# A transformer block in float32 on one core: the output projection regrouped into eleven matmuls a tile, with later weight splits

## The chip, the cores and the metric

The kernel runs on one core of one Trainium2 chip. The time is device microseconds of one launch, the median of three runs. One further launch was recorded by the hardware profiler; all rows below are of that one.

TensorE (PE) multiplies, VectorE (DVE) and ScalarE (ACT) do elementwise work, GpSimd (POOL) does small columns and issues accumulating DMAs, and SyncE (SP) issues the other DMAs. Each engine runs its own queue in the order in which the program was written.

## The reference

```python
x = A_x                                     # (1, 2048, 448), float32
mod = silu(c) @ w_mod                       # six rows of 448: sa, ca, ga, sb, cb, gb
h = layernorm(x) * (1 + ca) + sa
q, k, v = heads(h @ wqkv)                   # 16 heads of 28
pq, pk = phi(q), phi(k)                     # phi(t) = (t + 1 if t > 0 else exp(t)) + 1e-6
kv, z = einsum(pk, v), sum(pk)              # per head, over the 2048 tokens
o = (pq @ kv) / (pq . z + 1e-6)
x = x + ga * (o @ wo)
h = layernorm(x) * (1 + cb) + sb
u = gelu(layernorm(h).T @ w1 + b1)          # the MLP mixes tokens: w1 is 2048 x 1792
x = x + gb * (u @ w2 + b2).T                # w2 is 1792 x 2048
```

## The kernel before

The 2048 tokens are sixteen tiles of 128 rows. Everything is float32, but a matmul at full rate takes rounded operands. So an operand is split: a high part, rounded by ScalarE into a float32r tile, and a low part, the rest, by a VectorE subtraction. A product is then three matmuls: high by high, high by low, low by high.

**Stages.** First keys, queries and the sums over tokens, then a second loop over the tiles, then the rest of the MLP. The change is in the second loop and just ahead of it.

**Ahead of the loop.** The per-head matrices `kvm` (masked to the heads) times the four row groups `wo_sb[g]` of 112 rows give four products `wp` of 112 by 448, so that division by the denominator, `kv` and `wo` become one matrix. Each is split from PSUM into `wph` (ScalarE) and `wpl` (VectorE), eight tiles on 112 partitions.

**The loop.** It has `NT + LAG` = 21 iterations. Iteration `i` works on several tiles at once, in this order in the program (the function names are those of the code):

- TensorE: `b_transpose(i)` turns the normalised queries `pn` of tile `i` into a PSUM bank `tq`; `b_out(i-1)` is the output projection of the tile before, into `op`; `a_q` projects one or more of the queries still left (`QS` says how many in which iteration, one where it says nothing); `step(0, i-5)` is a piece of the first MLP matmul: four output tiles `up` by three matmuls.
- ScalarE and VectorE: `b_high(i)` and `b_low(i)` split `tq` into `pth` and `ptl`; `b_res(i-2)` adds `op` to x; `b_prod`, `b_sum`, `b_recip`, `b_scale` make `pn` of tile `i+1`; `b_norm1_a`, `b_norm1_b` (tile `i-3`) and `b_norm2` (tile `i-4`, which makes `y` and `h2h` on ScalarE) are the two layer norms; `b_mean1` and `b_mean2` are sums of squares on ScalarE (`sqa`, `sqb`); `b_low2` makes `h2l`; `a_phi_q` ends the queries with two activations and one VectorE operation.
- GpSimd: `nb` (in `b_norm2`), `nm` (`b_mean1`), `den` (`b_eps`), `ny` (`b_mean2`), and `b_rstd`, which is `vw` and the power `rt`, in that order within an iteration. `b_norm1_b` and `b_norm2` of the next iteration use `rt`.
- w1: `load_to` queues loads of 128 by 512 pieces `pr` on SP, `split_to` splits the next of them. A piece in `PIECE_DMA` is split without VectorE: ScalarE makes the high part `ph` and its negative in `pl`, and a GpSimd DMA adds the piece onto `pl`.

`step(0, t)` needs piece `t`; from iteration 17 on the loop also begins the next group of columns, with pieces 16 to 19. The tiles come from two pools of buffers, 74 in one and 27 in the other. The second holds among others the query weights (until the last `a_q`), `pd`, `pn`, the `wp` parts and the parts of pieces 9 to 11.

At the end of an iteration the program has:

```python
a_phi_q(nq)
load_to(14 + (i + 1) // 2)
split_to(10 + (i + 1) // 2)
if res or norm1:
    b_rstd(i, 0 if res else 1, 2 if norm1 else 1)
```

Of the kernel before, what the change touches and what calls it, by code (L numbers as in the profile page):

```python
# [8 lines left out]
F32 = mybir.dt.float32  # L9
F32R = mybir.dt.float32r  # L10
AF = mybir.ActivationFunctionType
# [3 lines left out]
P = 128  # L15
S, D, F = 2048, 448, 1792
NT = S // P
NF = F // P
G = 112
# [1 line left out]
DH = 28  # L21
EPS = 1e-5

PIECE_DMA = range(14, 18)
PRE_LOAD = {14: 2, 15: 4}
KV_LAG = 4
HIGH_AT = {13: (11, 12), 14: (13,), 15: (14, 15)}
# [10 lines left out]
CUT2 = {2: 9, 3: 9, 4: 8, 5: 7}  # L38
LAG = 5
MOD_AT = {9: [(4, 0)], 10: [(4, 1)], 11: [(4, 2)], 12: [(4, 3)], 13: [(3, 0)], 14: [(3, 1)]}  # L40
QS = {0: 2, 4: 2}
WARM = 9
PRE = 9
MID = 5
# [6 lines left out]
def block_kernel(ctx: ExitStack, tc: tile.TileContext, x, xt, wqkv, wo, w1, b1, w2, b2, c, wmod, wfirst, out):  # L51
    nc = tc.nc
# [15 lines left out]
    def slot(name, w=D, dt=F32, parts=P):  # L68
        return slots.tile([parts, w], dt, name=name, tag="slot", padded_shape=[P, 512])

    def tslot(name, dt=F32, parts=P, w=D):
        return tok.tile([parts, w], dt, name=name, tag="tok", padded_shape=[P, 512])


    def moving(new, name, dt=F32R, parts=P):
        return new(name, dt=dt, parts=parts, w=512)[:, 16:16 + D]
# [4 lines left out]
    def split(full, hi, lo):  # L81
        nc.scalar.activation(hi, full, AF.Copy)  # L82
        nc.vector.tensor_sub(lo, full, hi.bitcast(F32))  # L83
# [6 lines left out]
    ident = cst.tile([P, P], F32, name="ident")  # L90
# [103 lines left out]
    def mod_out(j, ps):  # L194
        mods[j] = cst.tile([P, D], F32, name=f"mod{j}")
        nc.scalar.activation(mods[j], ps[:, :D], AF.Copy, bias=1.0 if j == 4 else 0.0)
# [48 lines left out]
    def mod_sum2(j):  # L245
        ps = bank(f"modp{j}")
        hi, lo = macc.pop(j)
        nc.tensor.matmul(ps[:, :D], ones_r[:G, :], hi, start=True, stop=False)
        nc.tensor.matmul(ps[:, :D], ones_r[:G, :], lo, start=False, stop=True)
        return ps  # L250
# [46 lines left out]
    raws, parts = {}, {}  # L297
    done = {"load": 0, "split": 0}

    def load_to(i):  # L300
        while done["load"] < min(i, len(pieces)):
            k = done["load"]
            t, m, f0, n = pieces[k]
            raws[k] = slot(f"pr{k}", 512)
            nc.sync.dma_start(raws[k].rearrange("p (t f) -> p t f", t=m),
                              w1[t * P:(t + m) * P, f0 * P:(f0 + n) * P].rearrange("(t p) f -> p t f", p=P))
            done["load"] += 1

    def split_to(i):
        while done["split"] < min(i, len(pieces)):  # L310
            k = done["split"]
            new = tslot if k in TOKP else slot
            hi, lo = new(f"ph{k}", dt=F32R, w=512), new(f"pl{k}", dt=F32R, w=512)
            if k in PIECE_DMA:
                full = raws.pop(k)
                nc.scalar.activation(hi, full, AF.Copy)
                nc.scalar.activation(lo, hi.bitcast(F32), AF.Copy, scale=-1.0)
                nc.gpsimd.dma_start(lo, full, accum_op=ALU.add)
            else:
                split(raws.pop(k), hi, lo)  # L320
            parts[k] = (hi, lo)
            done["split"] += 1
# [64 lines left out]
    tps = {}  # L387
# [52 lines left out]
        nc.vector.scalar_tensor_tensor(dst, e, 1.0, r, op0=ALU.min, op1=ALU.add)  # L440
        return dst

    def phi_q(ps, t):
        dst, e, r = slot(f"pq{t}"), slot(f"eq{t}"), slot(f"rq{t}")
        nc.scalar.activation(e, ps, AF.Exp, scale=mv[t][:, 2:3])
        nc.scalar.activation(r, ps, AF.Relu, scale=mv[t][:, 2:3])
        nc.vector.scalar_tensor_tensor(dst, e, 1.0, r, op0=ALU.min, op1=ALU.add)
        return dst

    pq = [None] * NT  # L450
    qps = {}

    def a_q(t):
        project(t, 0, "qp")
        qps[t] = close(t, 0)
        del heads[t]

    def a_phi_q(keep=0):
        for t in sorted(qps)[:len(qps) - keep]:
            pq[t] = phi_q(qps.pop(t), t)  # L460


    xss, pks = {}, {}
# [267 lines left out]
    mp = mod_sum2(3)  # L731
    load_to(PRE + MID + 3)
    split_to(8)
    Wph, Wpl = [], []


    H2h, H2l = [None] * NT, [None] * NT
# [15 lines left out]
    def b_recip(t):  # L753
        nc.vector.reciprocal(dens[t], dens[t])

    def b_scale(t):
        pn = tslot(f"pn{t}")
        nc.vector.scalar_tensor_tensor(pn.rearrange("p (h d) -> p h d", d=DH),
                                       pq[t].rearrange("p (h d) -> p h d", d=DH), 1e-6,
                                       dens.pop(t).unsqueeze(2).to_broadcast([P, H, DH]),  # L760
                                       op0=ALU.add, op1=ALU.mult)
        pns[t] = pn
        pq[t] = None

    def b_transpose(t):
        pn = pns.pop(t)
        tps[t] = bank(f"tq{t}")
        for g in range(4):
            nc.tensor.transpose(tps[t][:G, g * P:(g + 1) * P], pn[:, g * G:(g + 1) * G], ident)  # L769

    def b_high(t):
        phs[t] = (slot(f"pth{t}", 512, F32R, parts=G), slot(f"ptl{t}", 512, F32R, parts=G))
        nc.scalar.activation(phs[t][0], tps[t][:G, :], AF.Copy)  # L773

    def b_low(t):
        nc.vector.tensor_sub(phs[t][1], tps.pop(t)[:G, :], phs[t][0].bitcast(F32))

    def b_out(t):
        ph, pl = phs.pop(t)
        opb[t] = bank(f"op{t}")  # L780
        n = 0
        for g in range(4):
            s = slice(g * P, (g + 1) * P)
            for a, b in ((ph, Wph[g]), (ph, Wpl[g]), (pl, Wph[g])):
                nc.tensor.matmul(opb[t][:, :D], a[:, s], b, start=(n == 0), stop=(n == 11))  # L785
                n += 1

    def b_sums(i):
        if i not in vss:
# [3 lines left out]
    def b_res(t):  # L793
        sums[t] = small.tile([P, 1], F32, name=f"sm{t}", tag="sm")
        nc.vector.scalar_tensor_tensor(X[t], opb.pop(t)[:, :D], 1.0, X[t], op0=ALU.mult, op1=ALU.add,
                                       accum_out=sums[t])
# [20 lines left out]
    def b_rstd(i, lo, hi):  # L817
        ve = small.tile([P, 2], F32, name=f"vw{i}", tag="vw")
        nc.gpsimd.tensor_scalar(ve[:, lo:hi], vss.pop(i)[:, lo:hi], 1.0 / D, EPS, op0=ALU.mult, op1=ALU.add)
        rss[i] = small.tile([P, 2], F32, name=f"rt{i}", tag="rt")  # L820
        nc.gpsimd.tensor_tensor(rss[i][:, lo:hi], ve[:, lo:hi], mhalf[:, lo:hi], op=ALU.pow)
# [10 lines left out]
    def b_low2(t):  # L832
        nc.vector.tensor_sub(H2l[t], ys.pop(t), H2h[t].bitcast(F32))
# [17 lines left out]
    for g in range(4):  # L851
        wp = bank(f"wp{g}")
        nc.tensor.matmul(wp[:G, :D], kvm[:, g * G:(g + 1) * G], wo_sb[g], start=True, stop=True)  # L853
        hi, lo = moving(tslot, f"wph{g}", parts=G), moving(tslot, f"wpl{g}", parts=G)
        split(wp[:G, :D], hi, lo)
        Wph.append(hi)
        Wpl.append(lo)
    mod_out(3, mp)

    accs, early = None, []  # L860
    for i in range(NT + LAG):
        if i == NT - 4:
            load_mod(5)
        if NT - 3 <= i <= NT:
            mod_part(5, i - NT + 3)
        if i == NT:
            mod_split(5)
        if i < NT:
            b_transpose(i)
        if 0 <= i - 1 < NT:  # L870
            b_out(i - 1)
        nq = min(len(late), QS.get(i, 1))
        for _ in range(nq):
            a_q(late.pop(0))
        t = i - LAG
        mp = mod_sum2(5) if i == NT else None
        if t >= 0:
            if t == 0:
                accs = [bank(f"up{f}") for f in range(4)]
            if i > NT:  # L880
                if not early:
                    early = [bank(f"up{W1G[1][0] + f}") for f in range(W1G[1][1])]
                r = i - NT - 1
                step(W1G[1][0], r, early, H2h[r], H2l[r])
            step(0, t, accs, H2h[t], H2l[t])
        if mp is not None:
            mod_out(5, mp)
        if i < NT:
            b_high(i)
        scale, res, norm1, norm2 = i + 1 < NT, 0 <= i - 2 < NT, 0 <= i - 3 < NT, 0 <= i - 4 < NT  # L890
        if res:
            b_res(i - 2)
        if scale:
            b_prod(i + 1)
        if norm2:
            b_norm2(i - 4, i)
        if res:
            b_mean1(i - 2, i)
        if norm1:
            b_norm1_a(i - 3)  # L900
        if scale:
            b_sum(i + 1)
        if norm1:
            b_norm1_b(i - 3, i)
        if scale:
            b_eps(i + 1)
        if i < NT:
            b_low(i)
        if norm1:
            b_mean2(i - 3, i)  # L910
        if scale:
            b_recip(i + 1)
        if scale:
            b_scale(i + 1)
        if norm2:
            b_low2(i - 4)
        a_phi_q(nq)
        load_to(14 + (i + 1) // 2)
        split_to(10 + (i + 1) // 2)
        if res or norm1:  # L920
            b_rstd(i, 0 if res else 1, 2 if norm1 else 1)

# [303 lines left out]
```

## Time and profile before

| | us |
|---|---|
| median of 3 runs | 444.76 (444.47 to 445.54) |
| the profiled launch, its own time | 445.22 |
| its span, first to last instruction | 443.5 |
| TensorE busy | 436.6 (98%), 2392 matmuls |
| VectorE busy | 364.7 (82%), 811 instructions |
| ScalarE busy | 273.3 (62%), 572 instructions |
| GpSimd busy | 110.0 (25%), 195 instructions |

The granted TensorE clock is at full speed in all of the span's forty slices. The second loop runs from 117.06 us, where tile 0 is transposed, to about 229 us, where the first four `up` are done. An engine's busy time counts instructions that overlap their neighbours at both ends, so what an engine needs is read from the distance between starts. An idle time of an engine that is not the one being waited for costs nothing.

### The profile page before, as it was taken

Reading aid. Unit: us, or ns where it says so; the run is one execution under the profiler, and the core shown is the slowest. Engines: PE = TensorE matmul, PEld = TensorE weight load, DVE = VectorE, ACT = ScalarE, POOL = GpSimd, SP = SyncE. Lnnn points to the kernel's source line nnn. Section 1 sums busy time; section 2 is a strip of 40 time slices with the busy share of each in tenths; the row PEclk is TensorE's granted clock in tenths of the full one; section 3 lists DMA queues with packets and bytes.
Section 4 is the critical chain, followed back from the end, with each engine's and each line's share of the span. In section 5 each row is a group of like instructions: output and inputs, shape, how many; then the busy total and the mean of one; then the engine's idle time right before and its main releaser. Section 6 shows DMA issues by size and latency. Waiting matters only on the chain.

```text
span 443.5 us, 7249 instructions
## 1 busy us (share of the span) xinstructions
PE 436.6 (98%) x2392; PEld 404.4 (91%) x2392; DVE 364.7 (82%) x811; ACT 273.3 (62%) x572; POOL 110.0 (25%) x195
## 2 busy tenths in 40 slices
PE   8999999999999999999999999999999999999995
PEld 7878899999899999989999999999999999999995
DVE  3989996689998899896468975829699998898892
ACT  3889877648656776767664354617375555645550
POOL 3227563200025355554300000010102331132010
PEclk9999999999999999999999999999999999999999
DMA  7998999545100004322328652478369978995332
GB/s 256 381 290 171 237 225 217 106 152 173 58 0 1 24 25 102 67 49 47 120 63 249 220 165 89 138 201 225 68 190 206 207 171 176 216 184 112 61 41 43
DMA packets 62294, 63.47 MB, mean 143 GB/s; under 512 B 4720, under 2 KB 54576, under 8 KB 62256
## 3 DMA queue, kind: packets, MB, share of 16 engines
q1 hardware_dynamic: 54048, 49.79, 37.3%
q0 software_dynamic: 8208, 13.21, 18.9%
q8 instruction: 19, 0.31, 0.3%
q14 instruction: 19, 0.16, 0.1%
HBM read 45.88 MB, written 7.34 MB: 120 GB/s over the span
## 4 chain that ended last, share of the span: by engine, by line
PE 93%; ACT 3%; DVE 2%; POOL 1%; issue 1%; ACTq 0%
PE y L1024 19%; PE up L838 10%; PE up L837 10%; PE up L836 9%; PE y L1025 9%; PE cacc L514 7%; PE qp L420 7%; PE op L785 7%; PE kp L420 6%; PE tq L769 1%; PE col L218 1%; PE warm L181 1%; PE qp L427 1%; PE kvb L725 1%; PE rowb L283 1%; PE wp L853 1%
## 5 line engine op out<-in xcount | busy, mean ns | idle before, releaser
L838 PE MATMUL up<-h2h,pl 128*128 128x448 f32 x224 | 81.4, 364 | 0.0
L837 PE MATMUL up<-h2l,ph 128*128 128x448 f32 x224 | 81.3, 363 | 0.0
L836 PE MATMUL up<-h2h,ph 128*128 128x448 f32 x224 | 80.9, 361 | 0.0
L986 POOL DMA_DIRECT2D a<-a x16 | 14.1, 960 | 142.7 <-DVE u L950 76.9
L837 PEld LDWEIGHTS up<-h2l,ph 128*128 128x128 f32 x224 | 42.1, 188 | 3.2
L836 PEld LDWEIGHTS up<-h2h,ph 128*128 128x128 f32 x224 | 42.0, 187 | 2.9
L838 PEld LDWEIGHTS up<-h2h,pl 128*128 128x128 f32 x224 | 42.1, 188 | 2.3
L83 DVE TENSOR_TENSOR pl<-pr,ph 128x512 fp32r<-128x512 f32 x52 | 34.6, 686 | 3.1 <-ACT ph L82 2.3
L82 ACT ACTIVATE ph<-pr 128x512 fp32r<-128x512 f32 x52 | 31.2, 626 | 3.3 <-PE up L837 2.6
L1030 ACT ACTIVATE cc<-y 128x448 f32<-128x448 f32 x24 | 12.9, 544 | 23.7 <-PE y L1025 23.7
L1044 POOL DMA_DIRECT2D out_dram<-yt x15 | 13.6, 908 | 48.6 <-DVE yt L1035 38.1
L514 PE MATMUL cacc<-pkh,xh 128*128 128x448 f32 x64 | 24.4, 382 | 0.3 <-ACT pkh L488 0.3
L785 PE MATMUL op<-wph,pth 112*128 112x448 f32 x64 | 24.5, 382 | 0.0
L950 DVE TENSOR_TENSOR u<-u,mod 128x448 f32<-128x448 f32 x14 | 8.7, 621 | 18.8 <-ACT u L949 18.6
L514 PE MATMUL cacc<-pkl,xh 128*128 128x448 f32 x64 | 23.3, 364 | 0.2 <-DVE pkl L490 0.2
L949 ACT ACTIVATE u<-up,b1c 128x448 f32<-128x448 f32 x14 | 8.7, 624 | 23.9 <-PE up L838 21.9
L420 PE MATMUL kp<-wh,hh 128*128 128x448 f32 x64 | 23.2, 373 | 0.2 <-ACT wh L256 0.2
L420 PE MATMUL qp<-wh,hh 128*128 128x448 f32 x64 | 23.3, 364 | 0.0
L785 PE MATMUL op<-wpl,pth 112*128 112x448 f32 x64 | 23.2, 363 | 0.0
L785 PE MATMUL op<-wph,ptl 112*128 112x448 f32 x64 | 23.2, 363 | 0.0
L773 ACT ACTIVATE pth<-tq 112x512 fp32r<-112x512 f32 x16 | 9.6, 598 | 17.3 <-PE tq L769 17.3
L827 ACT ACTIVATE y<-y,nb,rt 128x448 f32<-128x448 f32 x16 | 12.1, 758 | 11.8 <-POOL nb L826 11.8
(231 smaller groups left out, 1357.9 us busy)
## 6 DMA issues: line engine op xcount, KB each, us to landing
pr<-in_B_w_dram SPq DMA_DIRECT2D x56, 256.0 KB, 3.1
a<-in_B_w_dram SPq DMA_DIRECT2D x32, 256.0 KB, 4.8
a<-in_B_w_dram SPq DMA_DIRECT2D x32, 192.0 KB, 4.7
xt<-in_xt_dram SPq DMA_DIRECT2D x16, 256.0 KB, 4.8
x<-in_A_x_dram SPq DMA_DIRECT2D x16, 224.0 KB, 4.8
out_dram<-x SPq DMA_DIRECT2D x15, 224.0 KB, 2.5
out_dram<-yt POOLq DMA_DIRECT2D x15, 224.0 KB, 5.2
wm<-in_B_wmod_dram SPq DMA_DIRECT2D x16, 196.0 KB, 4.8
```

Of the source, the lines that this page charges most:

```text
L82: nc.scalar.activation(hi, full, AF.Copy)
L83: nc.vector.tensor_sub(lo, full, hi.bitcast(F32))
L420: nc.tensor.matmul(pps[t, j][:, :D], a[:, ch * P:(ch + 1) * P], w, start=first, stop=False)
L514: nc.tensor.matmul(cacc[ch][:, :D], a[:, s], b, start=(t == 0 and i == 0), stop=(t == NT - 1 and i == len(todo) - 1))
L785: nc.tensor.matmul(opb[t][:, :D], a[:, s], b, start=(n == 0), stop=(n == 11))
L836: nc.tensor.matmul(ps[:, :D], hi[:, sl], mh, start=first, stop=False)
L837: nc.tensor.matmul(ps[:, :D], hi[:, sl], ml, start=False, stop=False)
L838: nc.tensor.matmul(ps[:, :D], lo[:, sl], mh, start=False, stop=last)
L986: nc.gpsimd.dma_start(w, a, accum_op=ALU.add)
L1024: nc.tensor.matmul(ps[:, :D], h[:, s], w, start=opens and r == 0, stop=False, skip_group_check=True)
L1025: nc.tensor.matmul(ps[:, :HD], l[:, s], wh, start=False, stop=closes and r == PAIRS - 1, skip_group_check=True)
L1044: nc.gpsimd.dma_start(of[t * P:(t + 1) * P, :], ysum.pop(t), accum_op=ALU.add)
```

## The change

- **Products onto 128 partitions.** The 448 rows of the combined matrix are taken as three chunks of 128 rows and one of 64 instead of four of 112. `b_transpose` transposes chunks of 128, 128, 128 and 64 columns. The last chunk's high part stands on partitions 0 to 63 and its low part on 64 to 127 of the same columns, so that its high and low parts are multiplied in one matmul: eleven matmuls a tile instead of twelve.
- For that `b_high` and `b_low` become two instructions each (`b_low_last` is the second of VectorE's).
- **The combined matrix** is copied by ScalarE from PSUM into `wpg`, moved by eight SP DMAs between buffers into four tiles `wpr` with the new rows (the last 64 rows twice), and split from there in `wp_split`, at the end of iteration 0.
- **w1's pieces** are split later, and pieces 8 to 17 by DMA (14 to 17 before). One piece is split in each iteration from 6 on. Loads are as before up to iteration 15 and go further ahead after it.
- **Order:** `b_rstd` comes ahead of `split_to`; the queries' two activations come right after `b_high`, their VectorE operation at the end as before; three `a_q` in iteration 0 and one in iteration 4 (two and two before); `mod_sum2(5)` comes after `step` in iteration 16; `b_res(15)` comes in iteration 16.

```diff
-PIECE_DMA = range(14, 18)
+PIECE_DMA = range(8, 18)
-QS = {0: 2, 4: 2}
+QS = {0: 3}
...
     def b_transpose(t):
         pn = pns.pop(t)
         tps[t] = bank(f"tq{t}")
-        for g in range(4):
-            nc.tensor.transpose(tps[t][:G, g * P:(g + 1) * P], pn[:, g * G:(g + 1) * G], ident)
+        for ch in range(3):
+            nc.tensor.transpose(tps[t][:, ch * P:(ch + 1) * P], pn[:, ch * P:(ch + 1) * P], ident)
+        nc.tensor.transpose(tps[t][:64, 384:], pn[:, 384:D], ident)
 
     def b_high(t):
-        phs[t] = (slot(f"pth{t}", 512, F32R, parts=G), slot(f"ptl{t}", 512, F32R, parts=G))
-        nc.scalar.activation(phs[t][0], tps[t][:G, :], AF.Copy)
+        phs[t] = (slot(f"pth{t}", 512, F32R), slot(f"ptl{t}", 384, F32R))
+        nc.scalar.activation(phs[t][0][:, :384], tps[t][:, :384], AF.Copy)
+        nc.scalar.activation(phs[t][0][:64, 384:], tps[t][:64, 384:], AF.Copy)
 
     def b_low(t):
-        nc.vector.tensor_sub(phs[t][1], tps.pop(t)[:G, :], phs[t][0].bitcast(F32))
+        hi, lo = phs[t]
+        nc.vector.tensor_sub(lo, tps[t][:, :384], hi[:, :384].bitcast(F32))
+
+    def b_low_last(t):
+        ps, hi = tps.pop(t), phs[t][0]
+        nc.vector.tensor_sub(hi[64:, 384:], ps[:64, 384:], hi[:64, 384:].bitcast(F32))
 
     def b_out(t):
...
-        for g in range(4):
-            s = slice(g * P, (g + 1) * P)
-            for a, b in ((ph, Wph[g]), (ph, Wpl[g]), (pl, Wph[g])):
-                nc.tensor.matmul(opb[t][:, :D], a[:, s], b, start=(n == 0), stop=(n == 11))
-                n += 1
+        for ch in range(3):
+            s = slice(ch * P, (ch + 1) * P)
+            todo += [(ph[:, s], Wph[ch]), (ph[:, s], Wpl[ch]), (pl[:, s], Wph[ch])]
+        todo += [(ph[:, 384:], Wph[3]), (ph[:, 384:], Wpl[3])]
...
-        hi, lo = moving(tslot, f"wph{g}", parts=G), moving(tslot, f"wpl{g}", parts=G)
-        split(wp[:G, :D], hi, lo)
...
+        wpg = tslot(f"wpg{g}", parts=G)
+        nc.scalar.activation(wpg, wp[:G, :D], AF.Copy)
...
+                    nc.sync.dma_start(Wpr[ch][p0 + r0 - ch * P:p0 + r1 - ch * P], wpg[r0 - g * G:r1 - g * G])
+    mod_out(3, mp)
+
+    def wp_split(ch):
+        hi = moving(tslot, f"wph{ch}")
         Wph.append(hi)
-        Wpl.append(lo)
-    mod_out(3, mp)
+        Wpl.append(moving(tslot, f"wpl{ch}"))
+        split(Wpr[ch], hi, Wpl[ch])
...
-        mp = mod_sum2(5) if i == NT else None
...
             step(0, t, accs, H2h[t], H2l[t])
-        if mp is not None:
+        if i == NT:
+            mp = mod_sum2(5)
             mod_out(5, mp)
         if i < NT:
             b_high(i)
+        a_exp_q(nq)
-        if res:
+        if res and i < NT + 1:
             b_res(i - 2)
...
+        if i < NT:
+            b_low_last(i)
         if scale:
             b_scale(i + 1)
+        if i == NT:
+            b_res(i - 1)
         if norm2:
             b_low2(i - 4)
+        if i == 0:
+            for ch in range(4):
+                wp_split(ch)
         a_phi_q(nq)
-        load_to(14 + (i + 1) // 2)
-        split_to(10 + (i + 1) // 2)
+        load_to(max(14 + (i + 1) // 2, 12 + max(0, i - 6) + max(0, i - 14)))
         if res or norm1:
             b_rstd(i, 0 if res else 1, 2 if norm1 else 1)
+        split_to(8 + max(0, i - 5))
```

More of the change, by code (lines that the diff above doesn't have):

```diff
@@ L441, in phi_k, with q_exp, phi_q @@
         return dst
-    def phi_q(ps, t):
-        dst, e, r = slot(f"pq{t}"), slot(f"eq{t}"), slot(f"rq{t}")
+    eqs = {}
+    def q_exp(ps, t):
+        e, r = eqs[t] = (slot(f"eq{t}"), slot(f"rq{t}"))
         nc.scalar.activation(e, ps, AF.Exp, scale=mv[t][:, 2:3])
         nc.scalar.activation(r, ps, AF.Relu, scale=mv[t][:, 2:3])
+    def phi_q(t):
+        dst, (e, r) = slot(f"pq{t}"), eqs.pop(t)
         nc.vector.scalar_tensor_tensor(dst, e, 1.0, r, op0=ALU.min, op1=ALU.add)
@@ L456, in a_q, with a_exp_q @@
         del heads[t]
+    def a_exp_q(keep=0):
+        for t in sorted(qps)[:len(qps) - keep]:
+            q_exp(qps.pop(t), t)
     def a_phi_q(keep=0):
-        for t in sorted(qps)[:len(qps) - keep]:
-            pq[t] = phi_q(qps.pop(t), t)
+        a_exp_q(keep)
+        for t in sorted(eqs):
+            pq[t] = phi_q(t)
     xss, pks = {}, {}
@@ L733, in block_kernel @@
     split_to(8)
-    Wph, Wpl = [], []
+    Wpr, Wph, Wpl = [], [], []
     H2h, H2l = [None] * NT, [None] * NT
@@ L780, in b_out @@
         opb[t] = bank(f"op{t}")
-        n = 0
-        for g in range(4):
-            s = slice(g * P, (g + 1) * P)
-            for a, b in ((ph, Wph[g]), (ph, Wpl[g]), (pl, Wph[g])):
-                nc.tensor.matmul(opb[t][:, :D], a[:, s], b, start=(n == 0), stop=(n == 11))
-                n += 1
+        todo = []
+        for ch in range(3):
+            s = slice(ch * P, (ch + 1) * P)
+            todo += [(ph[:, s], Wph[ch]), (ph[:, s], Wpl[ch]), (pl[:, s], Wph[ch])]
+        todo += [(ph[:, 384:], Wph[3]), (ph[:, 384:], Wpl[3])]
+        for n, (a, b) in enumerate(todo):
+            nc.tensor.matmul(opb[t][:, :D], a, b, start=(n == 0), stop=(n == len(todo) - 1))
     def b_sums(i):
@@ L853, in block_kernel @@
         nc.tensor.matmul(wp[:G, :D], kvm[:, g * G:(g + 1) * G], wo_sb[g], start=True, stop=True)
-        hi, lo = moving(tslot, f"wph{g}", parts=G), moving(tslot, f"wpl{g}", parts=G)
-        split(wp[:G, :D], hi, lo)
+        wpg = tslot(f"wpg{g}", parts=G)
+        nc.scalar.activation(wpg, wp[:G, :D], AF.Copy)
+        if g == 0:
+            Wpr += [tslot(f"wpr{ch}") for ch in range(4)]
+        for ch in range(4):
+            r0, r1 = max(ch * P, g * G), min(ch * P + P, (g + 1) * G)
+            for p0 in (0, 64) if ch == 3 else (0,):
+                if r0 < r1:
+                    nc.sync.dma_start(Wpr[ch][p0 + r0 - ch * P:p0 + r1 - ch * P], wpg[r0 - g * G:r1 - g * G])
+    mod_out(3, mp)
+    def wp_split(ch):
+        hi = moving(tslot, f"wph{ch}")
         Wph.append(hi)
-        Wpl.append(lo)
-    mod_out(3, mp)
+        Wpl.append(moving(tslot, f"wpl{ch}"))
+        split(Wpr[ch], hi, Wpl[ch])
     accs, early = None, []
@@ L912, in block_kernel @@
             b_recip(i + 1)
+        if i < NT:
+            b_low_last(i)
         if scale:
             b_scale(i + 1)
+        if i == NT:
+            b_res(i - 1)
         if norm2:
             b_low2(i - 4)
+        if i == 0:
+            for ch in range(4):
+                wp_split(ch)
         a_phi_q(nq)
-        load_to(14 + (i + 1) // 2)
-        split_to(10 + (i + 1) // 2)
+        load_to(max(14 + (i + 1) // 2, 12 + max(0, i - 6) + max(0, i - 14)))
         if res or norm1:
             b_rstd(i, 0 if res else 1, 2 if norm1 else 1)
+        split_to(8 + max(0, i - 5))
     tok_ctx.__exit__(None, None, None)
```

## The prediction

> **What bounds the kernel now.** I read the page's busy times first, then who waited for whom from the loop on, then the chain of waits through the loop, and last the timeline of ScalarE and GpSimd beside it. The page says TensorE:
>
> ```profile
> span 443.5 us, 7249 instructions
> PE 436.6 (98%) x2392; PEld 404.4 (91%) x2392; DVE 364.7 (82%) x811; ACT 273.3 (62%) x572; POOL 110.0 (25%) x195
> ```
>
> The waits of TensorE from 117 us to the end hold one line (engine, waited for; us in total, times, longest):
>
> ```profile
> PE tq L769 <- DVE pn L758: 0.2, 1, 0.2
> ```
>
> So a matmul removed is time removed, as long as the other engines follow. The chain of waits gives the pace of the loop (start, us, what):
>
> ```profile
> 167.63 0.44 PE tq L769 x4
> 168.07 2.41 PE op L785 x12
> ...
> 178.15 0.44 PE tq L769 x4
> ...
> 199.37 0.62 PE tq L769 x4
> ```
>
> Tiles 9 and 11 are transposed at 167.63 and 178.15: 5.26 us an iteration. Four more would bring tile 15 to 199.19; it came at 199.37. So TensorE lost 0.18 us, all at the loop's end, and the wait was for VectorE's `pn`. What made that late is in the chain between tiles 14 and 15:
>
> ```profile
> 190.07 0.67 POOL nb L826
> 190.74 0.02 issue
> 190.77 0.77 ACT y L827
> 191.54 0.02 issue
> 191.56 0.58 ACT h2h L830
> 192.14 0.65 ACT sqa L330 x2
> 192.79 0.65 ACT sqb L330 x2
> 193.44 0.53 ACT ph L316
> 193.97 0.02 issue
> 194.00 0.64 ACT pl L317
> 194.64 0.40 issue
> 195.03 0.94 POOL pl L318
> 195.97 0.08 issue
> 196.05 0.19 POOL vw L819
> 196.25 0.07 issue
> 196.32 0.74 POOL rt L821
> ```
>
> This is a piece split by DMA. ScalarE does its norms, `ph` and `pl`; GpSimd starts the DMA 0.40 after `pl` ends, is held 0.94 by it, and only then does `vw` and `rt`, though `sqb`, which `vw` waits for, had long ended. Then the next round begins with `nb` and `y`. In the timeline, `y` of three rounds, and the `nb` of the last:
>
> ```profile
> 186.24 0.76 ACT L827 ACTIVATE y<-y,nb,rt 128x448 f32<-128x448 f32 x1 [1.76 <-POOL nb L826]
> ...
> 190.77 0.76 ACT L827 ACTIVATE y<-y,nb,rt 128x448 f32<-128x448 f32 x1 [1.02 <-POOL nb L826]
> ...
> 197.12 0.19 POOL L826 TENSOR_TENSOR nb<-ny,rt 128x1 f32<-128x1 f32 x1
> ...
> 197.35 0.76 ACT L827 ACTIVATE y<-y,nb,rt 128x448 f32<-128x448 f32 x1 [2.23 <-POOL nb L826]
> ```
>
> A round without a DMA takes 4.53, one with a DMA 6.58. They alternate, 5.55 on average against TensorE's 5.26, so the other engines fall behind by 0.3 an iteration in the second half, and the slack was just used up at tile 15. TensorE is the bound; this loop of ScalarE and GpSimd is second by a hair.
>
> **What the change does to TensorE.** Twelve `op` matmuls take 2.41, so 0.201 each. Sixteen tiles lose one each: 3.21 off. The four transposes stay four; `a_q` are as many as before, one of them in iteration 0 rather than 4. An iteration without `a_q` falls from 5.26 to 5.06. With the lost 0.18, at most 3.39 can be won: 445.22 - 3.39 = 441.83 for the profiled launch.
>
> **What it does to the second loop of engines.** From iteration 6 to 15 there is a DMA split in each iteration, ten in a row, not one in two. `vw` and `rt` go ahead of the DMA, so they run while ScalarE is at `ph` and `pl`: off the round. But the DMA now stands in GpSimd's queue ahead of the next iteration's `nb`, `nm` and `den`, and `y` waits for `nb`. The round, from the rows: `y` at 190.77 to the end of the hold at 195.97 is 5.20, then 0.08, `nb` 0.20 and 0.02, and `y` again: 5.50. That is better than 6.58 but it comes every time, and 5.50 is more than 5.06.
>
> When does it stop TensorE? `pn` of tile 15 needs `den`, which stands in GpSimd's queue behind the hold of iteration 13. The first hold is in iteration 6. Its end, from this row (before, the same in iteration 9, whose tile was transposed at 167.63):
>
> ```profile
> 172.96 0.96 POOL L318 DMA_DIRECT2D pl<-pr  x1 [2.39 <-ACT pl L317]
> ...
> 155.40 0.61 ACT L445 ACTIVATE eq<-qp,mv 128x448 f32<-128x448 f32 x1
> ```
>
> 173.92 - 167.63 = 6.29 after the transposes. In iteration 6 the last queries' two activations now stand ahead of `y` (two like the second row, 1.1 as they overlap a little), and `b_high` is two instructions instead of one: 0.1 more. So 7.5. Seven holds later, 38.5, the hold of iteration 13 ends. From `nb` (197.12) over `nm`, `den`, the reciprocal and `pn` to the transposes (199.37) it took 2.25; with 0.08 ahead and the new `b_low_last` in between, estimated at 0.2, it is 2.5. Tile 15's transposes so come 48.5 after tile 6's, where TensorE alone needs 9 x 5.06 = 45.5. **TensorE waits 3.0 in all**, from about tile 9 on, under half a microsecond a tile, before the transposes.
>
> After the last hold (iteration 15) rounds are of the 4.53 kind, and TensorE has two sets of twelve matmuls an iteration, 4.8, so it waits no more.
>
> **The rest, part by part.** VectorE per iteration, from one `x` to the next with no gap between, and its subtraction of `ptl`:
>
> ```profile
> 177.61 0.62 DVE L795 SCALAR_TENSOR_TENSOR x<-op,x 128x448 f32<-128x448 f32 x1
> ...
> 180.42 0.69 DVE L776 TENSOR_TENSOR ptl<-tq,pth 112x512 fp32r<-112x512 f32 x1
> ...
> 182.38 0.62 DVE L795 SCALAR_TENSOR_TENSOR x<-op,x 128x448 f32<-128x448 f32 x1
> ```
>
> It needs 4.77. The two subtractions in place of one cost between 0 and 0.69 more; I take 0.2, as the columns are the same: 4.97, under both 5.06 and 5.50, so it is covered by the round. The six splits that leave VectorE (0.69 each by the same width) cost nothing and win nothing here. ScalarE and GpSimd take them over: that is the round above. The pieces come eight iterations ahead of their use, so the later split itself stops nobody.
>
> The combined matrix's detour:
>
> ```profile
> 117.09 0.55 ACT L82 ACTIVATE wph<-wp 112x448 fp32r<-112x448 f32 x1 [0.21 <-PE wp L853]
> ...
> 109.07 2.03 SPq L305 DMA_DIRECT2D pr<-in_B_w_dram  x3
> ...
> wr<-in_qkv_dram SPq DMA_DIRECT2D x12, 224.0 KB, 5.3
> xpark<-x SPq DMA_DIRECT2D x1, 224.0 KB, 2.0
> ...
> 121.91 0.44 PE tq L769 x4
> ```
>
> The last copy ends at 117.64 as the last of `wph` did. SP is free (its loads ended at 111.1) and issues one DMA in 0.68, so the last of three starts at 119.0. No row shows a transfer between two buffers of the core; the nearest are a store, 2.0 to landing, and the slowest load, 5.3. I take 2.0, since no input is read from afar: 121.0, split by 122.2; at the worst 124.3 and 125.5. Before, tile 1 was transposed at 121.91; the third `a_q` of iteration 0 (eleven matmuls, 2.2) moves that to 124.1, `op` begins at 124.55 and uses the last chunk 1.8 later, 126.35. So 0 at both ends; with that cover gone each microsecond would cost one. The four VectorE splits move behind `pn` of tile 1 and delay nothing but an idle queue.
>
> `mod_sum2(5)` goes behind twelve matmuls (2.4), and ScalarE's copy of it stands ahead of `y` of tile 12: `y` is late, `h2l` of that tile is used in the next iteration behind twelve other matmuls. Between 0 and 0.6 (a ScalarE instruction); I take 0.2, since both come out within 0.3 of each other. `b_res(15)` earlier and the loads further ahead meet no wait of TensorE: 0.
>
> **The sum.** 445.22 - 3.21 - 0.18 + 3.0 + 0.2 = 445.03, 0.2 below the profiled launch. The median of the runs is 0.46 below that launch: 444.57, so **444.6**. What TensorE is spared it waits for. The measurement can tell about 0.3%, 1.33 us, from no change; the forecast is inside, its own range 443.4 to 446.0 (each 0.1 on the round is 0.7 over seven rounds).
>
> **Rivals.** *The full gain.* If the round comes out at 5.06 or less, TensorE stays the bound: 444.76 - 3.4 + 0.2 = 441.6. Needed is 0.45 off the round, for example that the 0.40 between `pl` and the DMA is hidden, now that GpSimd has just run `rt`. Against it: 0.40 stands behind `pl`, with GpSimd already idle, and would again. [...] 0.22.
>
> *Slower: `nb` is held in every round.* In the chain `nb` took 0.67, not 0.19, where it met a VectorE operation with two buffers as inputs:
>
> ```profile
> 190.00 0.68 DVE L805 SCALAR_TENSOR_TENSOR y<-x,nm,mod 128x448 f32<-128x448 f32 x1
> ```
>
> It ended with it, at 190.7. If each round falls so, it takes 5.97 and seven rounds 3.3 more: 447.9. It decides once VectorE's `b_norm1_b` runs later than the end of the hold; I put its end 0.4 ahead, in a VectorE that waits each round for `den`. The four extra `mod_part(5)` operations in iterations 13 to 16 push it that way, so a part of it is likelier than the whole. [...] 0.18.
>
> *The detour is late*, and `op` of tile 0 waits for `wph`: only beyond the 5.3 bound; 2 us late gives 446.6. 0.04.
>
> **Numbers.** Forecast 0.56; full gain 0.22, slower by `nb` 0.18, detour 0.04. Faster by over 0.3%: the full gain and the forecast's low edge, 0.25. Slower: the last two and its high edge, 0.24. Same 0.51. The range, 441.4 to 446.8, takes in the full gain and the late detour and reaches toward the slower rival; about 0.18 is left out, nearly all of it there.
>
> **What would show it.** `op` should have 176 matmuls instead of 192. `tq` should wait on `pn` by 0.3 to 0.5 from tile 9 or 10 to 15, about 3 us in all, and `tq` stand 5.5 apart there; GpSimd's DMA should be the step ahead of `nb`. No wait of `tq` and starts 5.06 apart would make the full gain right; starts 5.9 apart with `nb` at 0.6 the slower rival; an `op` waiting near 124.5 the detour.

## The result, and the profile after

| kernel | median of the runs, us | ratio to before | profiled launch, us | its span, us |
|---|---|---|---|---|
| before | 445.25 (444.47 to 445.61, 22 runs) | | 445.22 | 443.5 |
| after | 446.02 (445.39 to 447.79, 22 runs) | 1.0025 [1.0016, 1.0033] | 445.55 | 443.7 |

The changed kernel is 0.25% slower where 0.04% faster was forecast: both inside the 0.3% named as no change, but with the sign the other way, and the interval excludes no change. Two things make it up: the loop gained 0.5 us, a little more than forecast, and a place that the prediction did not look at, about 100 us behind the loop, lost 1.1 to 1.25.

The eleven matmuls, in the chain of waits of the kernel after (start, us, what):

```profile
123.75 0.33 PE tq L779 x3
124.08 0.11 PE tq L780
124.19 2.21 PE op L804 x11
```

2.21 where twelve took 2.41, and nothing waits at 124 for the combined matrix's detour. TensorE's instructions and its waits:

```profile
PE 434.0 (98%) x2376; PEld 399.7 (90%) x2376; DVE 363.9 (82%) x821; ACT 278.8 (63%) x598; POOL 112.2 (25%) x201
```

```profile
PE tq L779 <- DVE pn L768: 1.8, 6, 0.5
...
PE y L1062 <- DVE ut L83: 0.6, 1, 0.6
```

The first line is the wait that the prediction looked for, six times, 0.5 at the longest. Its cause is in the chain (two rounds of it):

```profile
156.75 0.96 POOL pl L318
157.71 0.24 POOL nb L844
157.96 0.03 issue
157.98 0.77 ACT y L845
...
161.21 0.63 ACT pl L317
161.84 0.39 ACT pth L784
162.23 0.03 issue
162.25 0.94 POOL pl L318
163.19 0.24 POOL nb L844
163.43 0.03 issue
163.46 0.77 ACT y L845
```

GpSimd's DMA is the step ahead of `nb`, as forecast, and `y` comes 5.48 later. Six such rounds after 157.98, `y` starts at 190.91: 5.49 each.

The second line, `y` for `ut`, is new; before had no wait of TensorE after the loop. It starts at VectorE, which takes a difference `s` of two blocks of w2, in two parts, ahead of the `u` that becomes `ut`. VectorE's timeline of before, and then of after (start, us):

```profile
316.11 0.69 DVE L992 TENSOR_TENSOR s<-a,a 128x512 f32<-128x512 f32 x1 [2.20 <-issue]
317.31 0.56 DVE L992 TENSOR_TENSOR s<-a,a 128x384 f32<-128x384 f32 x1 [0.51 <-DMA a<-a]
```

```profile
315.35 0.69 DVE L1030 TENSOR_TENSOR s<-a,a 128x512 f32<-128x512 f32 x1 [2.37 <-issue]
318.04 0.56 DVE L1030 TENSOR_TENSOR s<-a,a 128x384 f32<-128x384 f32 x1 [1.99 <-DMA a<-a]
```

The first part came 0.76 earlier, with the program; the second 0.73 later. It waits for the second of a pair of accumulating DMAs of GpSimd (a22 added onto a21, line 1024). The DMA view of that stretch, of before and of after (314 to 317.2, and 313.3 to 317.9; queue, packets, MB, share; then the one issue that falls into it, KB and time to landing):

```profile
q0 software_dynamic: 288, 0.46, 86.9%
issues: line engine op xcount, KB each, median us to landing
a<-a POOLq DMA_DIRECT2D x1, 192.0 KB, 3.9
```

```profile
q0 software_dynamic: 288, 0.46, 60.9%
q8 instruction: 1, 0.02, 2.1%
issues: line engine op xcount, KB each, median us to landing
a<-a POOLq DMA_DIRECT2D x1, 192.0 KB, 5.3
```

The same 288 packets, but after has one of queue 8 among them, kind "instruction": 16 KB in 1.54 us. In before it ran at 312.47, ahead of all packets of the pair. Queue 14, the only other one of that kind, has no packet between 307 and 320 us in either. The seven packets of queue 0 that after starts from 316.14 us on:

```profile
q0 software_dynamic: 7, 0.01, 4.7%
```

The other 281 had ended by 316.13. Queue 8's packet ended at 316.72, and these seven end one after another from 316.88 to 317.57; in before the last 24 packets of the pair end together, from 316.75 to 316.90.

### A table of where TensorE's time went

For each profiled kernel below, the start of one and the same matmul minus its start in before's profile. **Start** is that difference at the last `cacc` (102 us), where the sums over tokens end. **Loop** is what came on top from there to the 56th matmul of `y`, **step** what came on top from the 56th to the 112th (324 to 333 us). Behind it, up to TensorE's last matmul, the difference changes by no more than 0.02 in any kernel; in the profiles of mm_alone and late_dve the span ends 1.5 and 1.3 later still, behind that matmul. **Landing** is the second accumulating DMA's, issue to landing; **code** is the time of queue 8's packet and the number of TensorE instructions that the trace has before it (weight loads, matmuls and some 40 waits of its queue).

| kernel | start | loop | step | DMA issued, landing | code at, instruction |
|---|---|---|---|---|---|
| before | 0 | 0 | 0 | 313.35, 3.88 | 312.5, 3227 |
| after | -0.43 | -0.49 | +1.25 | 312.63, 5.33 | 315.2, 3235 |
| after_again | -0.35 | -0.50 | +1.09 | 312.60, 5.25 | 315.3, 3235 |
| defer | +0.33 | -3.41 | +1.10 | 310.23, 5.41 | 312.8, 3231 |
| nohold | +0.55 | -3.41 | +1.08 | 310.35, 5.50 | 313.0, 3231 |
| mm_alone | -0.03 | +1.30 | +1.22 | 314.37, 5.75 | 317.0, 3230 |
| late_dve | -0.25 | +0.40 | +1.52 | 313.60, 5.69 | 316.3, 3235 |
| before_shift | +0.73 | +0.08 | +1.31 | 314.66, 5.08 | 317.1, 3237 |
| after_pad | +4.69 | -0.17 | 0.00 | 317.43, 3.83 | 316.8, 3225 |
| defer_pad | +5.78 | -3.39 | 0.00 | 315.98, 3.85 | 314.7, 3227 |
| defer_pad_mod | +2.46 | -3.64 | 0.00 | 312.41, 3.84 | 311.1, 3225 |
| before_early | +0.02 | +0.05 | 0.00 | 310.34, 5.60 | 312.9, 3231 |
| after_early | -0.29 | -0.50 | -0.01 | 308.77, 5.34 | 314.6, 3225 |
| defer_mod_early | -0.05 | -3.62 | 0.00 | 306.42, 4.37 | 312.5, 3235 |

### The profile page after: what moved, and what is told of

It is laid out like the page before. It is cut to its first block, busy times and chain, and to the rows that moved or that the text cites. A ratio compares the mean times of both kernels' runs of the same rounds, so it can differ in the third digit from the quotient of the medians.

```text
span 443.7 us, 7292 instructions
## 1 busy us (share of the span) xinstructions
PE 434.0 (98%) x2376; PEld 399.7 (90%) x2376; DVE 363.9 (82%) x821; ACT 278.8 (63%) x598; POOL 112.2 (25%) x201
## 4 chain that ended last, share of the span: by engine, by line
PE 79%; ACT 10%; DMA 3%; DVE 3%; POOL 2%; issue 2%; SPq 0%; POOLq 0%; ACTq 0%; DVEq 0%
PE y L1062 16%; PE y L1063 8%; PE cacc L524 8%; PE up L856 8%; PE up L855 8%; PE up L854 8%; PE qp L420 7%; PE kp L420 6%; PE op L804 3%; POOL pl L318 2%; ACT y L845 1%; ACT sqa L330 1%; DMA a<-in_B_w_dram 1%; DMA a<-a 1%; ACT sqb L330 1%
## 5 line engine op out<-in xcount | busy, mean ns | idle before, releaser
L83 DVE TENSOR_TENSOR pl<-pr,ph 128x512 fp32r<-128x512 f32 x46 | 30.8, 686 | 4.1 <-ACT ph L82 3.3
L82 ACT ACTIVATE ph<-pr 128x512 fp32r<-128x512 f32 x46 | 27.6, 623 | 0.8 <-PE up L856 0.5
L804 PE MATMUL op<-wph,pth 128*128 128x448 f32 x64 | 24.5, 383 | 0.0
L804 PE MATMUL op<-wpl,pth 128*128 128x448 f32 x64 | 23.1, 362 | 0.0
L1062 PE MATMUL y<-ut,s1h 128*128 128x448 f32 x56 | 18.2, 376 | 0.6 <-DVE ut L83 0.6
L1030 DVE TENSOR_TENSOR a<-a,s 128x512 f32<-128x512 f32 (+1 forms) x32 | 18.4, 617 | 0.0
```

Of the source, the lines that this page charges most:

```text
L804: nc.tensor.matmul(opb[t][:, :D], a, b, start=(n == 0), stop=(n == len(todo) - 1))
L1030: nc.vector.tensor_tensor(w, raw2[q, a][i], raw2[q, b][i], op=op)
L1062: nc.tensor.matmul(ps[:, :D], h[:, s], w, start=opens and r == 0, stop=False, skip_group_check=True)
```

## The experiments

The ratios are to runs of before on the same chip in the same series (their medians: 445.21, 445.13 and 445.40). defer, nohold, after_again and mm_alone ran together, then the four with the warm-up changed, then late_dve with the last three.

### Is GpSimd's hold what TensorE waits for?

**defer.** The accumulating DMA of a piece is put off to the next iteration, behind that iteration's `nb`, `nm`, `den` and `ny`:

```diff
-                nc.gpsimd.dma_start(lo, full, accum_op=ALU.add)
+                lows.append((lo, full))
...
             b_mean2(i - 3, i)
+        add_lows()          # issues what lows holds
```

> The changed kernel with one move: the GpSimd DMA that ends a split is issued one iteration later, behind ny, so that it no longer stands ahead of nb. Theory A (the round of ScalarE and GpSimd, 5.5 us with the DMA's hold in it, costs TensorE 2.7 us in the loop, and the rest of the loss is at the start of the second MLP product): the round falls to about 4.5, tq waits for pn by less than 0.3 in all, tiles stand 5.06 apart, and the loop ends 2.5 earlier than in the changed kernel; if the later loss is chance of DMA landings, the kernel ends about 443.0 (1.005 times faster than before). Theory B (what is won before 315 us is lost again where the second MLP product begins, since transfers land there at their own pace): the loop gains as in A, but the wait at 320 to 333 us grows by as much, and the time stays at 445 to 446. Theory C (the loop's waits come from the two-instruction splits of tq on ScalarE and VectorE, not from the hold): no change, tq still waits 1.8 or more.

443.12 (442.70 to 444.08), ratio 0.9962 [0.9950, 0.9974]: faster than both kernels. The wait of `tq` is gone from TensorE's waits, and its transposes stand 5.05 apart in the chain:

```profile
156.23 0.33 PE tq L785 x3
156.56 0.11 PE tq L786
156.67 2.21 PE op L810 x11
...
161.28 0.33 PE tq L785 x3
```

The number of DMAs and the work of every engine are the same as in after; only the place in GpSimd's queue differs. The hold ahead of `nb` cost 2.9 us (the loop's -0.49 against -3.41).

**nohold.** The same DMAs left out instead of put off.

```diff
                 nc.scalar.activation(lo, hi.bitcast(F32), AF.Copy, scale=-1.0)
-                nc.gpsimd.dma_start(lo, full, accum_op=ALU.add)
```

> The changed kernel without the GpSimd DMAs of pieces 8 to 17 (the low parts of these pieces stay the negative of the high part, so that part of the first MLP product is left out); ScalarE's two activations stay. Theory A: the hold and the 0.4 ahead of it are gone from the round, which falls to about 4.2; tq waits under 0.3 in all; 442.5 to 443.0. Theory B: loop faster, same end, 445 to 446. Theory C: still 1.8 or more of waits of tq, no change.

443.18, a little above what was expected, ratio 0.9960 [0.9944, 0.9977], and a loop of -3.41, as in defer. So a DMA that stands behind `ny` costs TensorE nothing here: it is the order, not the transfer.

**after_again.** The kernel after, a second time.

> The changed kernel once more, for a second profile. Theory A and B: the loop shows the same rounds of 5.47 to 5.55 and 1.8 of waits of tq. If the loss at 318 to 333 us is chance of one DMA's landing (5.33 in the first profile against 3.88 before), it is another size here; if it stands, VectorE's second subtraction ahead of u again waits for that DMA by about 2 us and TensorE loses 1.2.

446.57, ratio 1.0035 [1.0022, 1.0048]; loop -0.50, step +1.09. Both parts repeat, the start's -0.4 less surely.

### What do the later splits and the splits by DMA do?

**mm_alone.** The eleven matmuls with before's splits:

```diff
-PIECE_DMA = range(8, 18)
+PIECE_DMA = range(14, 18)
-TOKP = range(9, 12)
+TOKP = range(10, 12)
-        load_to(max(14 + (i + 1) // 2, 12 + max(0, i - 6) + max(0, i - 14)))
+        load_to(14 + (i + 1) // 2)
+        split_to(10 + (i + 1) // 2)
         if res or norm1:
             b_rstd(i, 0 if res else 1, 2 if norm1 else 1)
-        split_to(8 + max(0, i - 5))
```

> The eleven matmuls with the detour of the combined matrix and the new order of the queries' activations, but w1's pieces split as before: when, by whom, and ahead of rstd (one tile more from the larger pool of buffers). Theory A: rounds with and without a DMA alternate as before (6.6 and 4.5), VectorE has half a split more an iteration; tq waits 1.8 to 2.2 in all, first at tile 11, and the kernel ends 1 us below before: 444.0 to 444.5. Theory B: 445 to 446 with a longer wait at the second product. Theory C: as the changed kernel, 446.

448.16, ratio 1.0070 [1.0056, 1.0084]: a miss of 4 us. Its loop is 1.8 longer than after's, and 1.6 of that is lost by the transposes of tile 6. The chain shows where; VectorE is on it in iterations 1 to 3:

```profile
123.71 0.63 DVE wpl L83
124.33 0.54 DVE pq L452
124.87 1.20 DVE pl L83 x2
126.07 0.55 DVE pd L754
...
128.23 0.63 DVE pn L768
128.86 1.61 DVE pq L452 x3
130.46 0.60 DVE pl L83
```

With the splits in their old place the `pl` of the early pieces meet the four `wpl` splits, which the change moved into the loop, and the queries' `pq`. So the later schedule is part of what the change needs; the prediction said of it only that it stops nobody. mm_alone also splits ahead of `b_rstd` and loads as before, which no run separates from the time of the splits.

**late_dve.** After, with its later schedule, but the low parts of pieces 8 to 13 by VectorE (`PIECE_DMA = range(14, 18)` alone).

> The kernel after with the low parts of pieces 8 to 13 taken by VectorE again, as in the kernel before (only 14 to 17 go by GpSimd's DMA); everything else as in after, the later splits too. Theory A (in after the rounds are set by GpSimd's hold of 0.92 to 0.96 us ahead of nb): without the holds the round is VectorE's own work, about 4.9 us (42.3 us busy in 8.7 rounds of the kernel without these DMAs) and 0.6 to 0.7 for a low part, 5.5 us, so the rounds of tiles 6 to 11 stay at about 5.5 us and the time at 446.0 to 446.6. If VectorE has more room than that: rounds of 5.1 us there, 444 to 445. If it has less: 447 or more.

446.98, ratio 1.0035 [1.0025, 1.0045]. The transposes of tiles 8 to 13 came 5.54 to 5.55 apart, the round that was expected from 4.9 of VectorE's own work and one low part; in the chain VectorE has taken GpSimd's place. VectorE is busy with no gap in such a round:

```profile
169.78 0.68 DVE y L827 x2
170.46 0.47 DVE ptl L789
...
171.44 0.62 DVE pn L768
172.06 0.54 DVE h2l L851
172.60 0.60 DVE pl L83
```

TensorE's waits begin at tile 8, two tiles sooner than in after, so that tile 15 comes 49.3 after tile 6 and not 48.4. The loop lost 0.9 against after, and the step is 0.3 larger: that is how it is past the 446.6 that was expected at most. In a round, one low part on VectorE costs about what the hold does on GpSimd (5.54 and 5.49); the DMA pays in full once it is behind `ny`.

### What is the loss 100 us behind the loop?

The theory here, called D: queue 8's packet loads TensorE's program, it does so at the same count of instructions in every kernel (column "code": 3225 to 3237), and so 16 matmuls and 16 weight loads fewer ahead of it put it 32 instructions later in the program, which is into the accumulating DMA. The trace of after has 18 packets of 16 KB on queue 8, the first at TensorE's instruction 180, the last at 4521, 255 apart on average. That they hold TensorE's program is inferred from this count: the profile gives only the queue and the kind "instruction".

**after_pad.** 32 TensorE instructions added, in the warm-up at the start:

```diff
-    keep_warm(WARM)
+    keep_warm(WARM - 2)
+    for _ in range(10):
+        nc.tensor.matmul(warm[:, :4], ones, ones[:, :4], start=True, stop=True)
```

> The changed kernel with 32 more TensorE instructions at the very start, where TensorE waits for inputs (ten matmuls of 4 columns in place of two of 128 in the warm-up; the arithmetic is the same). Theory D (TensorE's own code loading: it takes one 16 KB block about every 256 instructions; the block near instruction 3230 came at 312.5 before, ahead of the two accumulating DMAs that the second MLP product waits for, and since sixteen matmuls and sixteen weight loads are gone it comes in their midst, at 315.2): the block comes 3.2 us earlier in the program, the second accumulating DMA lands after 3.9 instead of 5.3, the step of 1.1 us between the first MLP product and the third group of the second is gone, and the median falls by 1.1 from 446.0-446.6 to 445.0-445.5. Theory E (that DMA is slow for where its buffers lie, or since everything ahead of it came earlier): no change, 446.0 to 446.6, and the second DMA takes 5.3.

449.85, ratio 1.0097 [1.0079, 1.0114]: in time a miss of more than 4 us. But the step is gone (0.00), and the landing is back at 3.83. What it lost it lost at the start, 4.69: the ten small matmuls took 4.27 us, and the sixteen `col<-sc,wm` after them 447 ns each (342 in before, 286 to 365 in the kernels with the old warm-up).

**before_shift.** The other way: before, with 32 fewer, by one warm-up matmul over 512 columns in the place of nine over 128.

```diff
-    keep_warm(WARM)
+    nc.tensor.matmul(warm, ones, ones[:, 0:1].to_broadcast([P, 512]), start=True, stop=True)
```

> The kernel before with 32 fewer TensorE instructions at the very start (one warm-up matmul of 512 columns in place of nine of 128), nothing else. Theory D: the code block moves into the accumulating DMAs as in the changed kernel; the second takes 5.3 instead of 3.9, TensorE waits about 0.5 at the second MLP product and the end comes 1.1 later, 446.3, ratio 1.0025. Theory E: no change, 445.2. If the shorter warm-up shows in the first stage, that is read off at the first keys and taken away.

447.95, ratio 1.0060 [1.0047, 1.0073], 1.6 above what was expected. The unchanged loop kept its pace (+0.08), and **the step appeared in the kernel before**: +1.31, landing 5.08. The start cost 0.73; the span is 2.2 longer, the median 2.8, and the other 0.6 lies outside the span.

**defer_pad** and **defer_pad_mod.** The same padding in defer; the second also with `mod_sum2(5)` at its old place ahead of the iteration's matmuls.

> The changed kernel with the GpSimd DMA of a split issued one iteration later, behind ny (443.12 by itself), and the 32 more TensorE instructions at the start. Theory D: the step of 1.1 at the second product is gone as well: 442.0. Theory E: 443.1.

> As the kernel with the DMA one iteration later and the 32 instructions, and mod_sum2(5) ahead of step again in iteration 16. The wait of 0.23 of TensorE for h2l of tile 12, which every kernel with the changed order shows, is gone: 0.2 below that kernel, 441.8; if that wait only covers another one, the same.

446.51 (442.94 to 448.49), ratio 1.0019 [0.9996, 1.0043], and 446.48 (443.80 to 447.68), ratio 1.0022 [1.0005, 1.0039]: misses of over 4 us, and spread wide. The step is 0.00 in both; what the runs pay is the start again, 5.78 and 2.46 in the profiles. defer_pad_mod also speaks against the second half of theory E: it issues the second of the pair at 312.41, sooner than after does (312.63), and the landing is 3.84. In defer_pad_mod the windows after the small matmuls show a lowered clock (us, engines busy, then granted clock, DMA share, GB/s):

```profile
6.50:9.00 2.50, 2.50 (x18) 2.19 (x17) 1.49 (x3) 0.63 (x1) 0.00 (x0) 0.78 1.01 360
9.00:11.80 2.80, 2.80 (x17) 1.88 (x15) 0.10 (x1) 0.00 (x0) 0.00 (x0) 0.58 1.03 383
```

In after_pad the windows show full clock there (1.00 in each from 4 to 16 us) and only the matmuls are longer, and before_shift, with no matmul of four columns, has the sixteen `col` at 446 ns too. So the runs do not show what made the start slow. As a cure for the step, padding at the start is no good.

**after_early.** A cleaner test: nothing added, but for the second pair of columns (`q == 1`) the blocks that are accumulated are loaded first, so the DMA pair can be issued 3.9 us sooner, ahead of the code.

```diff
-        for name, (fo, to) in QUADS.items():
+        for name in ("a21", "a22", "a11", "a12") if q == 1 else QUADS:
+            fo, to = QUADS[name]
```

> The kernel after, with one thing moved: for the second pair of output columns of the second MLP product (q = 1) the blocks a21 and a22 are loaded ahead of a11 and a12, so that GpSimd's two accumulating DMAs a<-a can be issued some 2 us sooner (before: 311.94 and 312.63 us in the trace of the kernel after). Theory D (the 16 KB of code for TensorE, loaded at instruction 3235, falls among the packets of the second accumulating DMA and delays it from 3.88 to 5.25 us or more, VectorE waits for it ahead of the next rows of u, and TensorE loses 1.1 to 1.26 us): both have landed before the code is loaded, the step between the 56th and the 112th matmul of y is gone, 445.0 to 445.5. Rival E (the step is not this DMA but something else in those microseconds, such as the order of VectorE's queue): no change, 446.0 to 446.6. If the loads of a11, now last, are late instead: 446 or more, with VectorE waiting for L1019 there.

445.34 (444.47 to 446.21), ratio 0.9999 [0.9990, 1.0008]; the step is -0.01. VectorE has the second part of `s` 3.9 us earlier:

```profile
313.31 0.69 DVE L1031 TENSOR_TENSOR s<-a,a 128x512 f32<-128x512 f32 x1
314.19 0.56 DVE L1031 TENSOR_TENSOR s<-a,a 128x384 f32<-128x384 f32 x1 [0.20 <-DVE s L1031]
```

The landing was 5.34 here too, with no code packet among its own but with the loads of a11 and a12 beside it (536 packets on queue 1). So the code is not the only thing that makes this DMA slow; what costs is that it lands too late for VectorE.

**before_early.** The same move in before.

> The kernel before, with the same move of the loads for q = 1. Theory D: TensorE lost nothing at this place in the kernel before (the code was loaded ahead of the accumulating DMAs' packets), so there is nothing to gain: 445.2, within 0.3 of the kernel before. If the move is a gain of its own, whatever the code does: 444.0 to 444.5.

445.21, ratio 0.9994 [0.9985, 1.0003], step 0.00. Here the code fell into the DMA (312.9; landing 5.60) and cost nothing, as the pair was issued 3 us sooner. The move is no gain of its own: what it brings in after (a ratio of 0.9999 for 1.0025) is the step.

**defer_mod_early.** The version that the runs point to: defer, `mod_sum2(5)` at its old place, and the loads of after_early.

```diff
+        mp = mod_sum2(5) if i == NT else None
         step(0, t, accs, H2h[t], H2l[t])
-        if i == NT:
-            mp = mod_sum2(5)
+        if mp is not None:
             mod_out(5, mp)
```

> The kernel after with the accumulating DMA of a piece's low part issued one iteration later (as in defer, 443.1), the modulation's sum put back to its place ahead of the iteration's VectorE work, and the loads of q = 1 in the order of after_early; no matmul is added. Theories A and D together: 443.1 less 0.2 for the order and 1.1 for the step: 441.6 to 442.0. If the step is not the accumulating DMA's lateness: 442.7 to 443.1.

**442.42 (441.87 to 443.02), ratio 0.9930 [0.9919, 0.9942]**, the fastest of all. Loop -3.62, step 0.00, and in the profile no wait of TensorE behind the first stage. The median lies between the two ranges that were expected, 0.4 above the first; but its ratio is 0.0032 below defer's, 1.4 us, where 1.3 was expected, and the runs of before were 0.2 slower in that series.

## Why the prediction was right or wrong

- **The matmuls, 3.21 and 0.18.** Right, though the 0.18 was read too small. It comes from pieces of the chain, which begin where the matmul ahead ends by the profile. By the transposes' own starts in the timeline (177.99 for tile 11, 199.37 for tile 15, 5.26 an iteration) TensorE lost 0.34 there, so that 3.55 could be won. Without a hold ahead of `nb` the loop gains 3.41 (defer, nohold, defer_pad), and 3.62 with the modulation's sum at its old place, against 3.39 forecast.
- **The round of ScalarE and GpSimd, 5.50, and TensorE's wait, 3.0.** Right: 5.49, and tile 15 is transposed 48.4 after tile 6 where 48.5 was forecast and defer takes 45.5: 2.9 (1.8 in the view of waits, which counts from the end of the matmul ahead, while a transpose that waits for nothing starts 0.16 before that end). defer shows that the hold is the cause. The first rival needed 0.45 off the round. In after the time between `pl` and the DMA stayed at 0.40 to 0.42 (161.84 to 162.25 in the rows above), and GpSimd was held for 0.92 to 0.96 in each round, worth 2.9 us in all. That rival's full gain in the loop came nevertheless in defer, but by another route: the order of the queue.
- **`mod_sum2(5)`, 0.2.** Right: 0.21 between the loops of defer and defer_mod_early, and about 0.2 in after, where two starts of `up` at 211.4 us are 0.31 apart instead of 0.20.
- **The six low parts "cost nothing and win nothing".** Half right. On VectorE they make a round as long as on GpSimd, but TensorE waits from two tiles sooner on, and the loop is 0.9 longer (late_dve). The later schedule, to which no price was given, keeps the early iterations from falling behind (mm_alone).
- **The slower rival, `nb` at 0.67 in every round.** It did not come: 0.24 in the rounds shown (0.55 once, at the loop's end), and no round near 5.97.
- **After the last hold TensorE "waits no more"**, and with it the sum's end at the loop. This step failed. The prediction added up the loop and let the rest ride along. TensorE lost 1.1 to 1.25 us at the start of the second MLP product, to a DMA that became 1.4 us slower. The sum should have been -0.5 + 1.2 = +0.7 for the medians (measured +0.77; in the profiled launches +0.33, as the changed kernel's start was 0.43 faster in that one). It is not the `op` matmuls being quicker, nor the splits, nor GpSimd's hold: the step is there in every kernel with 32 TensorE instructions fewer than before and the old order of loads, in before_shift too, and in none with the count restored. The prediction did not look at queue 8 at all. The profile of before had a warning at this place: VectorE already stood idle 2.20 and 0.51 ahead of the two parts of `s`, with little to spare behind them. In after the second part came 1.66 later against the program, and TensorE lost 1.25 of that, so 0.4 was spare. That 446.0 still lies within 441.4 to 446.8 is luck: that range was drawn for rivals that did not come.

How one packet of 1.5 us among 288 others delays the last of them can be seen in part. In each of the eight profiles in which it falls into the landing, seven to nine packets of the pair start only at its end and run one by one, 0.1 to 0.2 us apart, while the others are done. Why those were held back is not shown: the trace does not tell which DMA engine a packet used.

## What to carry to other kernels

The accumulating DMA that ends a split was an instruction of 0.92 to 0.96 us in GpSimd's queue here: put behind the small operations that others wait for, the same DMA was free (the loop gained 3.41 us with it in defer and without it in nohold). And when a change moves the number of TensorE's instructions, look past the place of the change for transfers that somebody barely waits for: queue 8's packets kept to the count of TensorE's instructions here (the thirteenth at 3225 to 3237) and so moved against everything else, and a transfer with no slack was better issued earlier (after_early, 445.34) than padded around (after_pad, 449.85). When two parts of a kernel's time move in opposite directions, compare the same matmul in both traces; the median alone, +0.8, hid -0.5 and +1.2.

## What the runs showed of the hardware

- Queue 8, kind "instruction", moved packets of 16 KB: 19 in before, of 0.88 to 1.42 us, and 18 in after, of 0.90 to 1.65, one for about 254 and 255 TensorE instructions; the thirteenth came at instruction 3225 to 3237 in all fourteen profiles. Where it fell between the issue and the landing of a 192 KB accumulating DMA, that took 5.08 to 5.75 us (eight profiles); where it ran ahead and the loads stood in the old order, 3.83 to 3.88 (four). In the eight, the last seven to nine packets of the DMA pair ran one by one behind that packet's end.
- Ten warm-up matmuls of four columns took 4.27 us in after_pad and 2.41 in defer_pad_mod, where nine of 128 columns took 3.78 in after. The sixteen matmuls behind took 447 ns each in after_pad and defer_pad and 361 in defer_pad_mod, 446 behind the one of 512 columns in before_shift, and 286 to 365 in the kernels with the old warm-up.
- In before the four `wp` matmuls, 448 columns with operands that were not rounded (`kvm`, `wo_sb`), took 3.00 us from the first start to the transposes behind them (113.89 to 116.89), two instructions each in the trace: 0.75 each. An `op` matmul of as many columns with rounded operands took 0.20 (twelve in 2.41).
